# Which of the free PSUM banks a product takes

## The chip, the cores and the metric

The kernel runs on one core of one Trainium2 chip. The metric is the device time of one execution in microseconds (us); the median of three runs is what a change is judged by. PE is TensorE's matmul stream, PEld its weight loads, DVE is VectorE, ACT is ScalarE, POOL is GpSimd, SP is SyncE, which issues nearly all DMAs. "L749" is line 749 of the kernel.

## The reference

A depthwise convolution over time with 7 taps, the tap weights a softmax shared by the 24 channels of each of 8 heads, is followed by RMS norm and a gated feed-forward layer. All is float32.

```python
x: (8, 4096, 192), weight: (8, 7), w_gate, w_val: (192, 1536), w_out: (1536, 192)
w = softmax(weight)                                  # over the 7 taps, per head
out[b, s, h, g] = sum_k w[h, k] * x_pad[b, s + k, h, g]    # 6 zero rows ahead of each batch row
x = out.reshape(32768, 192)
xn = x / sqrt(mean(x * x, -1) + 1e-6) * rms_g
g = xn @ w_gate
y = ((g * sigmoid(g)) * (xn @ w_val)) @ w_out         # (32768, 192)
```

## The kernel before

**Tiling.** The 32768 tokens are cut into 32 pairs of 2 x 512 tokens, each a stretch of 1024 tokens of one batch row. The hidden width of 1536 is cut into 4 units of 3 x 128 columns. The input products save multiplications by a Winograd-like scheme: sums of blocks of the input (XSUM, into the tile `xc`) and sums of blocks of the weights (WSUM, into `wf`) are multiplied, and the results are put together afterwards. The gate and the value matrices are worked on at once, on partitions 0 to 63 (half 0) and 64 to 127 (half 1) of the contraction; each product is one matmul on either half. The output products use a second scheme of this kind (OUTS) with three accumulators, X, Y and Z.

**Pair 0 and the others.** Pair 0 is computed plainly (`plain` and `outer`), while the weights are made ready. Pairs 1 to 31 are computed by the class `Pair`, and each of them goes through the same list of words, ORDER, written out by hand. The words set the order of the instructions on every engine: "p2" issues two more steps of PE's list of products, and a word such as "VR1.0.0" one operation: V, A, G and D stand for DVE, ACT, POOL and a DMA, R1 is the action, then half and unit. A "-" at the end means that the operation belongs to the pair before. So each engine's queue is fixed; the engines wait for each other by semaphores alone.

**The products of a unit.** PE's list for a pair is CHAINS, 240 matmul instructions of L749 (a float32 product takes two on each half), and then OUTS, 672 matmul instructions of L878. A unit has a number of running values v; each is accumulated in one PSUM bank per half. Three of them (4, 1, 5) are begun by a product[...]. The others (0, 2, 3) are begun by a fork ("F"): ACT or DVE copies value 1, 4 or 5 into another bank, and later products add to the copy. In unit 0 of a pair the first six products go to values 4, 1, 5, 4, 0, 4, in this order, on half 0 and half 1 in turn. The first reads block 5 of `xc`, the second block 9, the third a block of `xb` (the fetched input), the fourth `xc` block 4, the fifth block 7, the sixth block 8.

**Banks.** There are 8 PSUM banks of 512 columns, 4 for each half. For each half `free` lists the banks that are free, the one freed longest ago first. The set `whole` holds the banks that a matmul has written in all 512 columns since they were last begun. [...] The output accumulators X (half 0) and Z (half 1) are begun by matmuls that write 384 columns, so `open` strikes their banks off `whole`. `pick(h, full)` goes through the list for the first bank that is whole (or is not), and takes the first of the list if there is none:

```python
i = next((i for i in free[h] if ((h, i) in whole) == full), free[h][0])
```

A bank is given back when the last operation on it is issued: `leave` after a result (R, L773), a Silu (G) or a product with the gate (M); `part_tap` (L444) after the last tap of one of the three pieces of the convolution of a later pair, which run in PSUM too; `close` after Z is added to its tile (C21, L924), or after X or Y was transposed into the output tile (T12 and T11, two transposes each of L893). The instruction that next writes the bank waits for that operation.

**Where one pair meets the next.** The last DVE words of a pair are: C22 (L924, reads X at an earlier stage of its sum), the last tap of conv piece 1 (L444), T22, the block sum X2 (L667), C21 (the last reader of Z), a reduction of the norm (L470 to L472), the block sums X5, X8 and X10 (L667, into `xc` blocks 4, 7 and 9), T12. POOL's are the block sums X7, X3, X1, X6 (L667) and the norm's power (L476 to L482). Then come the next pair's first two product steps, and after them T11 (DVE, out of Y), and on POOL the block sums X9 and X4 of that pair (into `xc` blocks 8 and 3) and the norm's scaling (L497).

Of the kernel before, what the change touches and what calls it, by code (L numbers as in the profile page):

```python
# [19 lines left out]
def kernel(  # L20
# [650 lines left out]
    free = [[0, 1, 2, 3], [0, 1, 2, 3]]  # L671

    def bank(half, i):
        return ps[half * 4 + i]
# [4 lines left out]
    whole = {(h, i) for h in range(2) for i in range(4)}  # L679

    def pick(h, full):

        i = next((i for i in free[h] if ((h, i) in whole) == full), free[h][0])
        free[h].remove(i)
        return i
# [8 lines left out]
    def emit(until):  # L694
        while line and line[0][0] < until:
            heapq.heappop(line)[2]()
# [26 lines left out]
    class Unit:  # L723
# [3 lines left out]
            self.bk, self.tl = {}, {}  # L727

        def new(self, v, h, product=False):
            i = self.bk[v, h] = pick(h, not product)  # L730
            if product:
                whole.add((h, i))
            assert (h, i) in whole
            return bank(h, i)[:]
# [228 lines left out]
    def plain(hts):  # L963


        groups = [(u, g, f) for u in range(NU) for g in (1, 0) for f in range(NF)]
        groups[0 : 2 * NF] = [(0, g, f) for f in range(NF) for g in (1, 0)]
        held = {}

        def products():  # L970
            for u, g, f in groups:
                if len(hts) <= u:
                    hts.append(big.tile([P, 2, NF, T], F32, name="ht"))
                bks = held[u, g, f] = [free[h].pop(0) for h in range(2)]
                for k in range(KP):
                    for h in range(2):
                        nc.tensor.matmul(  # L977
                            out=bank(h, bks[h])[:], lhsT=wf[u][HALF[h], k * NF + f, :],
                            rhs=xb[HALF[h], g, k, :], start=(k == 0), stop=(k == KP - 1),
                            skip_group_check=True,  # L980
                        )
                yield

        def silus():
            for i in groups:
                sg = tiles.pop(0)
                nc.scalar.activation(out=sg[:], in_=bank(0, held[i][0])[:], func=AF.Silu)
                held[i].append(sg)
                yield

        def values():
            for u, g, f in groups:
                *bks, sg = held.pop((u, g, f))
                nc.vector.tensor_tensor(
                    out=hts[u][:, g, f, :], in0=bank(1, bks[1])[:], in1=sg[:], op=ALU.mult
                )
                tiles.append(sg)
                for h in range(2):
                    free[h].append(bks[h])
                yield  # L1000

        return products(), silus(), values()
# [118 lines left out]
    p, sl, v = plain(hts)  # L1121
# [44 lines left out]
    later(out_sums(), *[base + 2600 + 60 * i for i in range(4 * NM)])  # L1166
    emit(float("inf"))

    order = [w for row in ORDER for w in row.split()]
    past = None  # L1170
    for p in range(1, PAIRS + 1):
# [42 lines left out]
```

## Time and profile before

| | |
|---|---|
| median of 3 runs | 2642.21 us (2641.62 to 2646.78) |
| the profiled execution | 2638.08 us |
| its span, first to last instruction | 2636.2 us |
| granted TensorE clock | 0.997 of full |
| busy: PE, PEld | 2581.8 us, 1878.4 us |
| busy: DVE, POOL, ACT | 2271.7, 2091.1, 1614.4 us |
| L749 (input products) | 7440 matmul instructions, about 0.59 us each, overlapping |
| L878 (output products) | 17360 matmul instructions, 0.27 us (128 columns) or 0.38 us (256 columns) each, overlapping |

The page gives, for one execution, the busy time of each engine, the span in 40 slices, the chain of work that ended last, and the costliest groups of instructions. Matmuls are pipelined, so the durations of single ones overlap and their sum is more than the time; what matters is where PE stood idle and who ended the idle time. In the timeline a line gives the start, the busy time, the engine, the line, the operation, what it writes and reads, the shape, how many were merged ("x8"), and in square brackets the idle time ahead and the instruction that ended it. In the list of waits a line gives who waited for whom, the total in us, how many times, and the longest.

### The profile page before, as it was taken

Reading aid. Unit: us, or ns where it says so; the run is one execution under the profiler, and the core shown is the slowest. Engines: PE = TensorE matmul, PEld = TensorE weight load, DVE = VectorE, ACT = ScalarE, POOL = GpSimd, SP = SyncE. Lnnn points to the kernel's source line nnn. Section 1 sums busy time; section 2 is a strip of 40 time slices with the busy share of each in tenths; the row PEclk is TensorE's granted clock in tenths of the full one; section 3 lists DMA queues with packets and bytes.
Section 4 is the critical chain, followed back from the end, with each engine's and each line's share of the span. In section 5 each row is a group of like instructions: output and inputs, shape, how many; then the busy total and the mean of one; then the engine's idle time right before and its main releaser. Section 6 shows DMA issues by size and latency. Waiting matters only on the chain.

```text
span 2636.2 us, 71036 instructions
## 1 busy us (share of the span) xinstructions
PE 2581.8 (98%) x29002; PEld 1878.4 (71%) x29002; DVE 2271.7 (86%) x3606; ACT 1614.4 (61%) x2964; POOL 2091.1 (79%) x1693
## 2 busy tenths in 40 slices
PE   6999999999999999999999999999999999999998
PEld 3677777776777776777776777767777777777676
DVE  8988889888888888889888888888898888988875
ACT  5375556765556765557755567655577555676554
POOL 3987788877888777888787887777887778887776
PEclk9999999999999999999999999999999999999999
DMA  6312321323312223213233222233132232132210
GB/s 142 60 35 56 63 50 39 62 38 63 63 39 49 50 51 63 55 34 62 39 63 63 42 46 54 47 63 60 33 57 47 55 63 45 44 62 38 50 38 14
DMA packets 510660, 138.01 MB, mean 52 GB/s; under 512 B 482301, under 2 KB 484861, under 8 KB 510206
## 3 DMA queue, kind: packets, MB, share of 16 engines
q1 hardware_dynamic: 509772, 133.44, 26.7%
q8 instruction: 227, 3.72, 0.6%
q14 instruction: 101, 0.82, 0.1%
q10 hardware_dynamic: 560, 0.03, 0.0%
HBM read 83.87 MB, written 49.55 MB: 51 GB/s over the span
## 4 chain that ended last, share of the span: by engine, by line
PE 89%; DVE 6%; issue 2%; POOL 1%; SPq 1%; DMA 1%; ACT 0%; DVEq 0%; POOLq 0%
PE ps L749 61%; PE ps L878 27%; DVE xc L667 1%; DVE s L470 1%; DVE o_sb L893 1%; PE ps L977 1%; POOL wf L349 1%; DVE tls L924 1%; DVE y L444 0%; SPq L1115 0%; DMA x<-in_x_dram 0%; DVE y L405 0%; POOL wo_sb L311 0%; SPq L217 0%; DMA ht<-in_moe_w_val_dram 0%
## 5 line engine op out<-in xcount | busy, mean ns | idle before, releaser
L749 PE MATMUL ps<-xc,wf 64*128 64x512 f32 x4960 | 1249.7, 592 | 17.3 <-DVE o_sb L893 16.3
L749 PEld LDWEIGHTS ps<-xc,wf 64*128 64x128 f32 x4960 | 764.2, 186 | 319.5 <-issue 117.3
L749 PE MATMUL ps<-xb,wf 64*128 64x512 f32 x2480 | 707.7, 589 | 0.0
L705 ACT ACTIVATE tls<-ps 128x512 f32<-128x512 f32 (+1 forms) x636 | 365.6, 589 | 384.7 <-PE ps L878 204.0
L793 POOL TENSOR_TENSOR ht<-ht,tile 128x512 f32<-128x512 f32 x295 | 374.8, 1277 | 277.5 <-ACT tile L786 276.1
L705 ACT ACTIVATE tile<-ps 128x512 f32<-128x512 f32 x697 | 400.0, 594 | 277.2 <-PE ps L749 166.9
L749 PEld LDWEIGHTS ps<-xb,wf 64*128 64x128 f32 x2480 | 394.7, 187 | 138.4 <-issue 38.1
L705 ACT ACTIVATE ps<-ps 128x512 f32<-128x512 f32 (+1 forms) x651 | 366.9, 578 | 53.1 <-PE ps L878 38.8
L906 POOL TENSOR_TENSOR early<-ht 128x512 f32<-128x512 f32 x279 | 378.2, 1360 | 4.9
L793 POOL TENSOR_TENSOR ht<-ht,tls 128x512 f32<-128x512 f32 x201 | 254.9, 1275 | 72.4 <-ACT tls L786 70.5
L878 PE MATMUL ps<-ht,wo_sb 128*32 128x256 f32 (+1 forms) x6944 | 308.7, 326 | 0.0
L773 DVE TENSOR_TENSOR tile<-ps,tile 128x512 f32<-128x512 f32 x373 | 255.0, 687 | 56.1 <-PE ps L749 53.5
L444 DVE SCALAR_TENSOR_TENSOR ps<-xh,tp,ps 128x512 f32<-128x512 f32 x435 | 301.7, 746 | 1.0
L878 PEld LDWEIGHTS ps<-ht,wo_sb 128*32 128x32 f32 x6944 | 215.0, 110 | 93.0 <-POOL ht L793 23.5
L878 PE MATMUL ps<-ht,x 128*32 128x256 f32 (+1 forms) x5952 | 249.2, 326 | 0.2 <-issue 0.2
L906 POOL TENSOR_TENSOR ht<-ht 128x512 f32<-128x512 f32 x186 | 247.5, 1345 | 0.0
L786 ACT ACTIVATE tile<-tile 128x512 f32<-128x512 f32 x373 | 232.9, 629 | 12.5 <-DVE tile L773 12.5
L878 PEld LDWEIGHTS ps<-ht,x 128*32 128x32 f32 x5952 | 191.7, 110 | 52.1 <-issue 0.7
L773 DVE TENSOR_TENSOR ht<-ps,tls 128x512 f32<-128x512 f32 x311 | 212.0, 682 | 0.0
L773 DVE TENSOR_TENSOR ht<-ps,tile 128x512 f32<-128x512 f32 x309 | 210.5, 681 | 0.0
L773 DVE TENSOR_TENSOR tls<-ps,tls 128x512 f32<-128x512 f32 x247 | 169.5, 686 | 28.2 <-PE ps L749 26.1
L878 PE MATMUL ps<-early,x 128*32 128x256 f32 (+1 forms) x4464 | 192.8, 326 | 0.0
(129 smaller groups left out, 3167.2 us busy)
## 6 DMA issues: line engine op xcount, KB each, us to landing
xb<-xd SPq DMA_DIRECT2D x124, 384.0 KB
xd<-yn SPq DMA_DIRECT2D x248, 96.0 KB
out_dram<-o_sb SPq DMA_DIRECT2D x186, 128.0 KB
xh<-in_x_dram SPq DMA_DIRECT2D x192, 105.0 KB
xh<-in_x_dram SPq DMA_DIRECT2D x56, 98.4 KB
ht<-in_moe_w_gate_dram SPq DMA_DIRECT2D x12, 192.0 KB
ht<-in_moe_w_val_dram SPq DMA_DIRECT2D x12, 192.0 KB
tls<-in_moe_w_out_dram SPq DMA_DIRECT2D x8, 192.0 KB
```

Of the source, the lines that this page charges most:

```text
L349: nc.gpsimd.tensor_tensor(out=t[:, d, :], in0=t[:, a, :], in1=t[:, b, :], op=ALU.add if op == "add" else ALU.subtract,)
L444: nc.vector.scalar_tensor_tensor(out=dst, in0=xk, scalar=w, in1=at, op0=ALU.mult, op1=ALU.add)
L470: nc.vector.tensor_reduce(out=ss[:], in_=sq, axis=AX.X, op=ALU.add)
L667: e.tensor_tensor(out=xc[:, d, :], in0=x_op(a), in1=x_op(b), op=ALU.add)
L705: nc.scalar.activation(out=dst, in_=src, func=AF.Copy, scale=float(s))
L749: nc.tensor.matmul(out=self.new(v, h, True) if first else self.old(v, h), lhsT=wf[self.u][HALF[h], WAT[i], :], rhs=x_op(XOP[i])[HALF[h]], ...
L773: nc.vector.tensor_tensor(out=self.hv(v) if h else t[:], in0=self.old(v, h), in1=t[:], op=plus(s))
L786: nc.scalar.activation(out=t[:], in_=src[:], func=AF.Silu)
L793: engine[eng].tensor_tensor(out=self.hv(v), in0=src, in1=t[:], op=ALU.mult)
L878: nc.tensor.matmul(out=self.bank(b)[i * Q : (i + 1) * Q, at : at + n], lhsT=left, rhs=cols, start=fresh, stop=True, skip_group_check=True, ...
L893: nc.vector.transpose(out=to[:, n, lo:hi], in_=src[:, lo * Q : hi * Q].rearrange("p (b e) -> p b e", e=Q),)
L906: engine[eng].tensor_tensor(out=dst, in0=a, in1=b, op=op)
```

## The change

A product that begins value 4 or 1 takes the head of the free list, whatever is marked. A product that begins value 5 goes on looking for a bank that isn't whole; so do the output accumulators X and Z and the pieces of the convolution, which call `pick` themselves. Forks go on asking for a whole bank. Once, after pair 0 and ahead of pair 1, the free lists are sorted so that the banks that are not whole stand first; the order within the two groups stays.

```diff
@@ class Unit
         def new(self, v, h, product=False):
-            i = self.bk[v, h] = pick(h, not product)
+            if product and v != 5:
+                i = free[h].pop(0)
+            else:
+                i = pick(h, not product)
+            self.bk[v, h] = i
             if product:
                 whole.add((h, i))
             assert (h, i) in whole
@@ ahead of the loop over the pairs
     later(out_sums(), *[base + 2600 + 60 * i for i in range(4 * NM)])
     emit(float("inf"))
 
+    for h in range(2):
+        free[h].sort(key=lambda i: (h, i) in whole)
     order = [w for row in ORDER for w in row.split()]
     past = None
     for p in range(1, PAIRS + 1):
```

## The prediction

> **What bounds the kernel now.** I read the page first, then TensorE's list of waits, then the timelines of TensorE (PE), its weight loads (PEld), VectorE (DVE) and GpSimd (POOL) around two borders between pairs: one near 303 us, one near 382 us.
>
> ```profile
> span 2636.2 us, 71036 instructions
> ...
> PE 2581.8 (98%) x29002; PEld 1878.4 (71%) x29002; DVE 2271.7 (86%) x3606; ACT 1614.4 (61%) x2964; POOL 2091.1 (79%) x1693
> ```
>
> PE is busy for all but 54 us. A gain must come out of those 54 us, or from shorter matmuls, which the change does not touch. The list of what PE waited for (total, times, longest):
>
> ```profile
> PE ps L749 <- DVE o_sb L893: 16.3, 19, 0.9
> ...
> PE ps L878 <- issue: 1.7, 4, 1.0
> ```
>
> The first line is the only wait that recurs in the steady loop: a matmul of line 749 waits for a transpose of line 893. The large remaining waits (15.7, 5.5 and 3.0 us, each once) are in the start. PE's timeline at a border that waits and at one that doesn't:
>
> ```profile
> 300.12 2.13 PE L878 MATMUL ps<-ht,wo_sb 128*32 128x256 f32 x48
> 303.16 1.99 PE L749 MATMUL ps<-xc,wf 64*128 64x512 f32 x8 [0.90 <-DVE o_sb L893]
> ...
> 382.63 1.99 PE L749 MATMUL ps<-xc,wf 64*128 64x512 f32 x8
> ```
>
> Reading the idle time ahead of the first L749 matmul at all 30 borders from the same view: 18 have 0.81 to 0.94 us (16.1 us in all), one 0.20, three 0.04 to 0.06, eight nothing; sum 16.4 us. A border without a wait comes mostly 79.47 us after the one ahead, a border with one about 80.45 us. DVE just ahead of both borders:
>
> ```profile
> 294.59 0.56 DVE L924 TENSOR_TENSOR tile<-ps,tile 128x384 f32<-128x384 f32 x1 [2.31 <-PE ps L878]
> ...
> 296.27 1.72 DVE L667 TENSOR_TENSOR xc<-xb,xc 128x512 f32<-128x512 f32 x1
> ...
> 301.77 0.69 DVE L667 TENSOR_TENSOR xc<-xc 128x512 f32<-128x512 f32 x1
> 302.38 1.16 DVE L893 STREAM_TRANSPOSE o_sb<-ps 128x256 f32<-128x256 f32 x4
> 306.12 0.69 DVE L769 TENSOR_TENSOR tls<-ps,tls 128x512 f32<-128x512 f32 x1 [2.58 <-PE ps L749]
> ...
> 375.04 0.56 DVE L924 TENSOR_TENSOR tile<-ps,tile 128x384 f32<-128x384 f32 x1 [1.06 <-PE ps L878]
> ...
> 376.72 0.71 DVE L667 TENSOR_TENSOR xc<-xb,xc 128x512 f32<-128x512 f32 x1
> ...
> 381.82 0.63 DVE L893 STREAM_TRANSPOSE o_sb<-ps 128x256 f32<-128x256 f32 x2
> ```
>
> At 294.59 DVE has waited for PE's bank X; then it has a fixed row of work that ends with T12, the transpose out of X. Of the four transposes at 302.38 two are T12; at 381.82 they stand alone and take 0.63, so T12 ends at 303.01. PE was ready at 303.16 - 0.90 = 302.26. The waiting border is 1.0 us later because one sum (X2) takes 1.72 instead of 0.71 us. POOL shows why:
>
> ```profile
> 296.15 1.29 POOL L667 TENSOR_TENSOR xc<-xb,xc 128x512 f32<-128x512 f32 x1
> ...
> 376.82 1.76 POOL L667 TENSOR_TENSOR xc<-xb,xc 128x512 f32<-128x512 f32 x1
> ```
>
> Whichever of the two sums starts first runs at its own pace, the other is held.
>
> [...] the third product's load (304.52) is 0.43 us ahead of its matmul (304.95).
>
> **The change, part by part.** I followed both free lists through a pair. On half 0 a pair starts with banks last freed by unit 3's R2, by conv piece 0, by conv piece 2 and by T12 (bank X, the only one not whole); on half 1 with those freed by R2, by conv piece 1 and by C21 (bank Z, not whole), and T11's a little later.
>
> 1. *Before*, every product prefers the bank that isn't whole: product 4, the first matmul of the pair, takes X on half 0 and so waits for T12, the latest event of all. *After*, product 4 takes R2's bank, product 1 the conv piece's, product 5 takes X and Z. Fork 0 takes what it took. From there on all banks are whole, both rules take the head of the list, and each later bank has the same releaser as before: only bank numbers differ. So six bank choices per border move, 30 times; no matmul, copy, transpose or DMA is added, removed or moved in any queue.
>
> 2. *The wait removed.* R2's bank was freed tens of us earlier. Removed: all 16.4 us.
>
> 3. *Where the stall goes: product 5.* Its first matmul is third product, 1.79 us after the first (304.95 - 303.16), and its weight load, where a wait can hold it, 1.39 us after:
>
> ```profile
> 303.13 0.33 PEld L749 LDWEIGHTS ps<-xc,wf 64*128 64x128 f32 x4 [1.14 <-issue]
> 303.67 0.22 PEld L749 LDWEIGHTS ps<-xc,wf 64*128 64x128 f32 x2 [0.21 <-issue]
> 304.10 0.22 PEld L749 LDWEIGHTS ps<-xc,wf 64*128 64x128 f32 x2 [0.21 <-issue]
> 304.52 0.22 PEld L749 LDWEIGHTS ps<-xb,wf 64*128 64x128 f32 x2 [0.21 <-issue]
> ```
>
> With the first product at 302.26 the load comes at 303.65. T12 ends at 303.01 and was seen by the load at 303.13, so 0.52 us are left: cost 0. If T12 were later than that, every product queued behind on PE, and through them ACT's copies, would slip by the difference.
>
> 4. *What is late next: X10.* Product 1 reads xc's slot 9, which X10 (301.77, just ahead of T12) writes. Until now the wait for T12 covered it. It ends at 302.46 and is visible at 302.58; product 1's load comes at 302.26 + (303.67 - 303.13) = 302.80. 0.22 us left: cost 0, and the thinnest cover.
>
> 5. *Further on.* The sixth product reads what POOL's next sum writes (303.73 + 1.26 = 304.99); it starts at 302.26 + 5 x 0.86 = 306.56, its load 0.43 earlier: 1.1 us left. T11's bank is free at 303.54, ahead of the end of product 1 on which fork 0 waits. DVE waits 2.58 us for PE at 306.12, so it still falls in step with PE, 0.9 us earlier. POOL's chain shrinks from a 0.88 us wait to none, and its next wait is 5.0 us. All three follow PE, so the gain stays.
>
> 6. *Waits to be added.* One wait at product 4 becomes up to three (products 4, 1, 5). A separate semaphore instruction on PE takes 51 ns in this trace: from 0 to 30 x 3 x 0.05 = 4.6 us. The loads sit idle 0.21 us between one another: I take 0.
>
> 7. *The sort.* At pair 1 the lists are 3, 1, 2, 0 with only 3 whole; sorted they are 1, 2, 0, 3, which gives pair 1 the banks it had. Host work: 0.
>
> Sum: -16.4 us against the profiled execution's 2638.08 us (span 2636.2), so about 2621.7 there. That execution is 4.1 us below the median shown, so against the median: 2642.2 - 16.4 = 2625.8, said as 2626. Differences under 0.2% (5.3 us) can hardly be told from no change.
>
> **Unknown at both ends.** Four pairs lose about 1 us to "issue" in the output products (the second wait line; those pairs take 80.45 to 80.8 us with no or almost no wait at the border). Two of them follow the 8 borders without a wait, two the 18 with one. If the rate without waits (1 in 4) holds for all, it is 7.5 instead of 4: +3.5 us; if they vanish, -4 us.
>
> **Rivals.**
> - *The wait comes back in part* at product 1 or 5, because DVE has drifted by more than 0.22 or 0.52 us. [...] At 0.2 to 0.5 us in 20 pairs it gives back 4 to 10 us: 2630 to 2636.
> - *The wait moves elsewhere in the pair*, DVE or POOL setting the pace: 2640 to 2643. For it: DVE 86%, POOL 79% busy. Against: both wait for PE in every pair, and seven borders already come 79.5 us after the one ahead with no wait at either place.
> - *Slower:* PE, never pausing at the border, outruns its instruction supply in the output products. Place: line 878; price about 1.0 us a time, 4 times in 30 now. It cancels the gain at 16 more pairs and is slower by 0.2% from 22 more: all 26 remaining ones would give about 2652. For it: the small excess noted above; against: 18 pauses of 0.9 us didn't prevent it either.
> - That the change doesn't do what it says would need X to be whole when product 4 picks; opening X always strikes it off, so I give this nothing apart.
>
> **How the numbers follow.** Full gain 0.80 (own range 2622 to 2630), partial 0.08, moved 0.06, slower 0.06. Faster by over 0.2%: 0.88, within: 0.06, slower: 0.06. The range 2622 to 2636 takes in the full gain with both ends of the unknowns and most of the partial case.
>
> **What would show it.** Right: no L749 wait on L893 left; every border 79.5 us apart save a few with "issue"; X2 still 1.72 us in many pairs without effect; PE busy as before, span about 2620. Wrong at step 3: L749 waits on L893 at the third product. Wrong at step 4: L749 waits on L667. Wrong at step 5: new PE waits inside the pair. The prediction fails if DVE at the border comes over 0.5 us later relative to PE than in this trace.

## The result and the profile after

Median 2624.88 us (2624.07 to 2626.45, four runs) against 2641.91 us of the kernel before on the same chip: ratio 0.9932, 95% interval 0.992 to 0.9943, 17.0 us less. Run again beside later experiments: 2624.53 against 2643.72 us, ratio 0.9925 (0.9909 to 0.9942). The profiled execution took 2624.07 us, 14.0 us less than that of before.

In the changed kernel the lines behind the edit stand four further down: L749 is L753, L878 is L882, L893 is L897, L924 is L928. L882, as L878 before, is 20832 matmul instructions (672 in each of 31 pairs); the 17360 of the table above leaves out its smaller groups. First the head of the page after:

```profile
span 2622.2 us, 71005 instructions
...
PE 2579.8 (98%) x29002; PEld 1858.8 (71%) x29002; DVE 2268.0 (86%) x3606; ACT 1614.9 (62%) x2964; POOL 2091.7 (80%) x1693
```

PE's busy time is within 2 us of what it was (2581.8); the span is 14.0 us shorter. In the list of PE's waits (total, times, longest) these are all that is left of L753 and L882:

```profile
PE ps L882 <- issue: 1.9, 5, 0.8
...
PE ps L753 <- DVE xc L667: 0.9, 1, 0.9
```

The wait for the transposes, 16.3 us in 19 places, is gone altogether, and no other that recurs has come in (the one wait for L667 stood in the list before too, with 0.8 us). The chain that ended last says the same. By engine, before:

```profile
PE 89%; DVE 6%; issue 2%; POOL 1%; SPq 1%; DMA 1%; ACT 0%; DVEq 0%; POOLq 0%
```

and after:

```profile
PE 95%; POOL 1%; DMA 1%; DVE 1%; SPq 1%; issue 0%; ACT 0%; DVEq 0%; POOLq 0%
```

At the borders DVE has left the chain: its 6% was the way from C22's wait through T12 to product 4, and nearly all that is left of it lies in the start. Now a border at which the sum X2 takes 1.73 us, one of POOL's sums having begun 0.11 us ahead of it (a held border, from here on; at the six borders where X2 starts 0.08 to 0.13 us ahead of that sum it takes 0.67 to 0.73 us), in PE's timeline, then in that of the weight loads:

```profile
301.80 1.70 PE L882 MATMUL ps<-ht,wo_sb 128*32 128x128 f32 x40
303.43 1.99 PE L753 MATMUL ps<-xc,wf 64*128 64x512 f32 x8
305.25 1.02 PE L753 MATMUL ps<-xb,wf 64*128 64x512 f32 x4
306.11 1.45 PE L753 MATMUL ps<-xc,wf 64*128 64x512 f32 x6
```

```profile
303.43 0.30 PEld L753 LDWEIGHTS ps<-xc,wf 64*128 64x128 f32 x4 [0.20 <-issue]
303.97 0.19 PEld L753 LDWEIGHTS ps<-xc,wf 64*128 64x128 f32 x2 [0.23 <-DVE xc L667]
...
304.83 0.19 PEld L753 LDWEIGHTS ps<-xb,wf 64*128 64x128 f32 x2 [0.24 <-DVE o_sb L897]
```

Product 1's load (303.97) now names X10, and product 5's (304.83) names T12, as the prediction worked out. Both come at their due times, by which I mean the times at which they come when nothing holds them: 0.54 and 1.40 us after the first product. So neither waits; idle times of 0.23 and 0.24 us are the stream's usual ones. At all 30 borders these loads come within 0.01 us of these times. DVE and POOL there:

```profile
295.84 0.56 DVE L928 TENSOR_TENSOR tile<-ps,tile 128x384 f32<-128x384 f32 x1 [2.30 <-PE ps L882]
...
297.53 1.73 DVE L667 TENSOR_TENSOR xc<-xb,xc 128x512 f32<-128x512 f32 x1
...
303.04 0.69 DVE L667 TENSOR_TENSOR xc<-xc 128x512 f32<-128x512 f32 x1
303.65 1.16 DVE L897 STREAM_TRANSPOSE o_sb<-ps 128x256 f32<-128x256 f32 x4
306.42 0.69 DVE L773 TENSOR_TENSOR tls<-ps,tls 128x512 f32<-128x512 f32 x1 [1.61 <-PE ps L753]
```

```profile
297.42 1.29 POOL L667 TENSOR_TENSOR xc<-xb,xc 128x512 f32<-128x512 f32 x1
...
307.46 2.92 POOL L497 TENSOR_TENSOR yn<-y,s 128x1536 f32<-128x1536 f32 x1
```

X2 still takes 1.73 us and T12 is as late as ever: it ends at 303.65 + 0.63 = 304.28, now 0.85 us *after* the first product. DVE's next wait for PE is 1.61 us (2.58 before), POOL's wait of 0.88 us ahead of L497 is used up, and its next one is 4.93 us (5.01 before).

Where the 14.0 us of the profile come from: the waits at the borders are worth 16.4 us; 2.1 us are lost again in the start, and 0.3 us, on balance, elsewhere. The start, up to the first L753 matmul at 142.9 us (140.8 before), lies ahead of all the bank choices that changed. In the ten profiles of the experiments it takes 141.9 to 143.4 us under either rule, so the early start belongs to that one execution of the kernel before and not to the rule. The medians differ by 17.0.

### The profile page after: what moved, and what is told of

It is laid out like the page before. It is cut to its first block, busy times and chain, and to the rows that moved or that the text cites. A ratio compares the mean times of both kernels' runs of the same rounds, so it can differ in the third digit from the quotient of the medians.

```text
span 2622.2 us, 71005 instructions
## 1 busy us (share of the span) xinstructions
PE 2579.8 (98%) x29002; PEld 1858.8 (71%) x29002; DVE 2268.0 (86%) x3606; ACT 1614.9 (62%) x2964; POOL 2091.7 (80%) x1693
## 4 chain that ended last, share of the span: by engine, by line
PE 95%; POOL 1%; DMA 1%; DVE 1%; SPq 1%; issue 0%; ACT 0%; DVEq 0%; POOLq 0%
PE ps L753 62%; PE ps L882 33%; POOL wf L349 1%; PE ps L981 1%; DMA xh<-in_x_dram 0%; SPq L1119 0%; SPq L217 0%; DMA x<-in_x_dram 0%; POOL wo_sb L311 0%; DVE y L420 0%; DMA ht<-in_moe_w_val_dram 0%; DVE xc L667 0%; DVE ht L998 0%; DMA ht<-in_moe_w_gate_dram 0%; POOL xc L310 0%
## 5 line engine op out<-in xcount | busy, mean ns | idle before, releaser
L753 PE MATMUL ps<-xc,wf 64*128 64x512 f32 x4960 | 1253.8, 592 | 0.9 <-DVE xc L667 0.9
L753 PEld LDWEIGHTS ps<-xc,wf 64*128 64x128 f32 x4960 | 753.5, 186 | 315.5 <-issue 92.9
L753 PE MATMUL ps<-xb,wf 64*128 64x512 f32 x2480 | 711.2, 589 | 0.0
L753 PEld LDWEIGHTS ps<-xb,wf 64*128 64x128 f32 x2480 | 389.7, 187 | 146.5 <-issue 41.1
L882 PE MATMUL ps<-ht,wo_sb 128*32 128x256 f32 (+1 forms) x6944 | 309.5, 326 | 0.0
L882 PEld LDWEIGHTS ps<-ht,wo_sb 128*32 128x32 f32 x6944 | 215.2, 110 | 93.2 <-POOL ht L797 22.7
L882 PE MATMUL ps<-ht,x 128*32 128x256 f32 (+1 forms) x5952 | 249.9, 326 | 0.6 <-issue 0.6
L882 PEld LDWEIGHTS ps<-ht,x 128*32 128x32 f32 x5952 | 190.1, 110 | 54.7 <-issue 2.3
L882 PE MATMUL ps<-early,x 128*32 128x256 f32 (+1 forms) x4464 | 193.1, 326 | 0.1
```

Source lines behind the costliest of these rows:

```text
L753: nc.tensor.matmul(out=self.new(v, h, True) if first else self.old(v, h), lhsT=wf[self.u][HALF[h], WAT[i], :], rhs=x_op(XOP[i])[HALF[h]], ...
L882: nc.tensor.matmul(out=self.bank(b)[i * Q : (i + 1) * Q, at : at + n], lhsT=left, rhs=cols, start=fresh, stop=True, skip_group_check=True, ...
```

## The experiments

Each time is set against the kernel before on the same chip. Where the changed kernel did not run beside it, "over the changed kernel" sets the distances of the two from the kernel before side by side.

**One half at a time: h0_only and h1_only.** The new rule on one half of the banks, the old one on the other.

```diff
-            if product and v != 5:
+            if product and v != 5 and h == 0:     # h0_only; h == 1 in h1_only
```

> The new rule on half 0 only; on half 1 every product prefers the bank that is not whole, as before, so its product 4 takes Z. My theory (the wait is for T12, on X's bank, half 0): the whole gain, 16 to 17 us below the kernel before, no L749 wait on L893 (here a shifted line). Rival A (the gain comes from Z and half 1): no change. Rival B (the gain comes from spreading the products over banks in general): about half, 8 us.

> The new rule on half 1 only; on half 0 product 4 still takes X. My theory: no change against the kernel before (within 1 us), 18 or 19 waits for T12's transposes, some 16 us. Rival A: the whole gain, 17 us. Rival B: about 8 us.

Measured: half 0 alone 2625.75 against 2644.89 us, ratio 0.9927 (0.9911 to 0.9944), 19.1 us less, and no wait of L753 for L897. Half 1 alone 2643.98 us, ratio 1.0 (0.9992 to 1.0009), with this line in PE's list of waits (23 where my theory had 18 or 19; five of them are under 0.75 us):

```profile
PE ps L753 <- DVE o_sb L897: 18.9, 23, 0.9
```

The whole gain lies on half 0, in X's bank and T12. Z's bank and C21, which half 1 concerns, are worth nothing that can be measured, and so is spreading the products over the banks on that half; early_before, below, has the gain with no spreading at all. Both kernels keep the sort of the free lists, so h1_only shows that the sort alone is worth nothing either.

**How late T12 may be: x_to_1.** Product 1 takes X's bank, 0.86 us earlier than product 5.

```diff
-            if product and v != 5:
+            if product and v != 1:
```

> Product 1 instead of product 5 takes the bank that is not whole; 4 and 5 take the head of the list. Product 1's weight load comes 0.54 us after the first product, T12 is visible 0.87 to 0.97 us after it in the 14 to 18 borders with the held sum. My theory: 0.33 to 0.43 us of wait there, 5 to 8 us of the gain lost: 9 to 12 us below the kernel before. Rival C (it is enough that the first product doesn't take X): the whole gain, 17 us. Rival D (T12 is late by far more than 0.5 us once PE no longer waits for it): more than 10 us lost.

Measured 2628.19 us (2624.72 to 2631.08), ratio 0.9935 (0.992 to 0.9949): 16.7 us below the kernel before. My theory's loss of 5 to 8 us did not come; by the ratio nearly the whole gain is there, as rival C had it. The median is still 2.4 us above that of h0_only on this chip; the trace has 0.7 us of loss at the borders and 7.0 us of "issue" waits, against 4.8. The wait that my theory spoke of is in the trace. Weight loads, then matmuls, at a held border:

```profile
782.68 0.30 PEld L753 LDWEIGHTS ps<-xc,wf 64*128 64x128 f32 x4 [0.20 <-issue]
783.58 0.30 PEld L753 LDWEIGHTS ps<-xc,wf 64*128 64x128 f32 x4 [0.60 <-DVE o_sb L897]
```

```profile
782.68 2.03 PE L753 MATMUL ps<-xc,wf 64*128 64x512 f32 x8
784.54 1.02 PE L753 MATMUL ps<-xb,wf 64*128 64x512 f32 x4
```

Product 1's load comes 0.90 us after the first product instead of 0.54, and is held by T12. Yet the third product starts 1.86 us after the first, where the changed kernel has 1.82: of 0.36 us, 0.04 remain. When nothing holds them the loads run 0.43 us ahead of their matmuls (product 5's in the changed kernel 1.39 and 1.82 us after the first product), and the two passes of a product (its first and its second matmul on each half) have a load each (x2), 0.43 us apart. When the first load is held, the loads of both passes go out together (x4 in 0.30 us), and the matmul doesn't need the old lead: it starts 0.07 us into a load of 0.18 us. In the traces of four_after and x1_twice, below, load and matmul of the held product start together (787.60 and 787.60, 784.40 and 784.40).

**T12 twice: twice_after and twice_before.** T12's transposes are issued twice, so X's bank is free one repeat later.

```diff
-                self.turn(self.bank(b), 0, int(act[2]) - 1)
+                for _ in range(2 if b == "X" else 1):
+                    self.turn(self.bank(b), 0, int(act[2]) - 1)
                 self.close(b)
```

> The changed kernel with T12's two transposes issued twice (the same values written again), so X's bank is free about 0.58 us later. My theory: in the borders with the held sum T12 is visible 1.45 to 1.55 us after the first product, product 5's load comes at 1.39: 0.06 to 0.16 us in 14 to 18 borders, 1 to 3 us over the changed kernel, 14 to 16 us below the kernel before. Rival D (there is no spare time at product 5): 0.58 us in 14 to 30 borders, 8 to 17 us over the changed kernel.

> The kernel before with T12's two transposes issued twice. My theory (product 4 waits for T12 with no spare time): 0.53 to 0.58 us at all 30 borders, 16 to 17 us slower than the kernel before. Rival E (DVE catches the lost time up elsewhere in the pair, or the wait seen at the border is only partly T12's): under 8 us.

The changed kernel with it: 2624.28 us, ratio 0.992 (0.9905 to 0.9935), no loss: product 5's load is held past its due time at 14 borders, by 0.07 us at most, and no product is late for it. My theory's 1 to 3 us did not come, nor rival D's 8 to 17. The kernel before with it: 2659.18 against 2642.35 us, ratio 1.0064 (1.0049 to 1.0079), 16.8 us slower, and all 30 borders wait:

```profile
PE ps L749 <- DVE o_sb L893: 33.5, 30, 1.5
```

The same 0.53 us of DVE work at the same place costs 0.56 us a border under the old rule (16.8 / 30; 0.43 to 0.70 by the interval) and nothing that can be measured under the new one. That is the change in one comparison, and rival E is out.

**T12 earlier: early_before and early_after.** T12 moves up in DVE's order, ahead of X8 and X10, under either rule.

```diff
-        ... VX5 p2 VX8 p2 VX10 p1 Gpow VT12 p2
+        ... VX5 p2 VT12 VX8 p2 VX10 p1 Gpow p2
```

> The kernel before with T12 moved up in DVE's order, from behind X10 to behind X5; the old bank rule. T12 then ends near 301.75 on the scale of the border at 303 us, ahead of PE's 302.26: product 4 waits no more. X8 and X10 end 0.58 us later, X10 visible at about 303.1, product 1's load at 302.80. My theory: 0.3 to 0.4 us of wait for L667 at 18 borders, 5 to 7 us of the gain missing: 10 to 12 us below the kernel before. Rival F (the wait at product 4 is for something else that ends together with T12): no change. Rival G (X10 has ample time): the whole gain, 17 us.

> The changed kernel with T12 moved up in the same way. My theory: product 5 has no need of it, and X10, now later, holds product 1: the same time as the kernel before with T12 moved up (within 1 us), so 5 to 7 us over the changed kernel, 10 to 12 us below the kernel before. Rival G: the time of the changed kernel.

Measured 2626.68 against 2642.35 us, ratio 0.9938 (0.9922 to 0.9955), with the old rule; 2624.90 us, ratio 0.9936 (0.9921 to 0.9951), with the new one. The two are the same within 2 us, as my theory had it, but at the level of the changed kernel, not 5 to 7 us above. No wait for L893 is left with the old rule, so it was T12 and nothing else that product 4 waited for: rival F is out. Weight loads, then matmuls, of early_before at a held border:

```profile
303.03 0.30 PEld L749 LDWEIGHTS ps<-xc,wf 64*128 64x128 f32 x4 [0.20 <-issue]
303.88 0.31 PEld L749 LDWEIGHTS ps<-xc,wf 64*128 64x128 f32 x4 [0.55 <-DVE xc L667]
```

```profile
303.03 1.99 PE L749 MATMUL ps<-xc,wf 64*128 64x512 f32 x8
304.86 1.02 PE L749 MATMUL ps<-xb,wf 64*128 64x512 f32 x4
```

X10 does hold product 1's load, for 0.31 us over its due time (0.85 instead of 0.54), and again the products after it are not late: the third starts 1.83 us after the first, where the changed kernel has 1.82, and no border of either kernel loses more than 0.03 us. So moving one operation in DVE's order does what the change does: what matters is that the *first* product needn't wait. It has no load running ahead that could absorb a wait (its load and its matmul start together, 303.43 and 303.43 in the changed kernel).

**The size of what is absorbed: after_again, four_after, x1_twice.** Two kernels in which the hold is long enough to cost, with the changed kernel beside them. four_after is twice_after with `range(4 ...`; x1_twice is twice_after with `v != 1`.

> The changed kernel itself once more, as the base for the two beside it: 16 to 18 us below the kernel before.

> The changed kernel with T12's two transposes issued four times (the same values written again): each repeat adds 0.53 us, so T12 is visible 2.56 us after the first product in the held borders, 1.54 in the others; product 5's weight load is due at 1.39, its matmul at 1.82. Theory H (a late weight load is absorbed for about 0.40 us, since the load is issued ahead of its matmul): 0.77 us of wait at some 18 borders, none at the others: 12 to 15 us over the changed kernel. Theory I (the wait costs from the load's due time on, as worked out in the prediction): 1.17 us at 18 borders and 0.15 at the others: 21 to 24 us over the changed kernel.

> Product 1 takes X's bank (product 5 the head of the list), and T12's transposes are issued twice: visible 1.51 us after the first product in the held borders, 0.48 in the others; product 1's weight load is due at 0.54, its matmul at 0.96. Theory H: 0.57 us at some 18 borders, 9 to 11 us over the changed kernel. Theory I: 0.97 us at some 18 borders, 16 to 18 us over the changed kernel, no better than the kernel before.

Against 2643.72 us before: the changed kernel 2624.53, four_after 2639.61 (ratio 0.9983, 0.9977 to 0.999), x1_twice 2637.70 (0.9977, 0.9968 to 0.9986); 15.1 and 13.2 us over the changed kernel. For four_after that is at the edge of theory H and far below theory I; for x1_twice it lies between the two, 2 us above H and 3 below I. The traces decide. PE at a held border of four_after, with the load that it waits for:

```profile
785.13 1.99 PE L753 MATMUL ps<-xc,wf 64*128 64x512 f32 x8
787.60 1.13 PE L753 MATMUL ps<-xb,wf 64*128 64x512 f32 x4 [0.48 <-DVE o_sb L897]
788.56 1.88 PE L753 MATMUL ps<-xc,wf 64*128 64x512 f32 x8
```

```profile
787.60 0.30 PEld L753 LDWEIGHTS ps<-xb,wf 64*128 64x128 f32 x4 [1.31 <-DVE o_sb L897]
```

Product 5's load goes out 2.47 us after the first product instead of 1.39, 1.08 late; the fourth product (788.56) comes at 3.43 instead of 2.68 (306.11 - 303.43), 0.75 late. The sixth is 0.75 late too. So 0.33 us are absorbed. In x1_twice:

```profile
783.00 1.13 PE L753 MATMUL ps<-xc,wf 64*128 64x512 f32 x4
784.40 1.13 PE L753 MATMUL ps<-xc,wf 64*128 64x512 f32 x4 [0.27 <-DVE o_sb L897]
785.37 1.02 PE L753 MATMUL ps<-xb,wf 64*128 64x512 f32 x4
```

```profile
784.40 0.30 PEld L753 LDWEIGHTS ps<-xc,wf 64*128 64x128 f32 x4 [1.10 <-DVE o_sb L897]
```

the load comes 1.40 us after the first product instead of 0.54, 0.86 late, and the products from the third on 0.54: 0.32 absorbed. With x_to_1 (0.36 late, 0.04 left) that is the same figure three times, and all the traces agree: of the 119 loads of products 1 and 5 that X10 or T12 held by over 0.02 us in these kernels, the 43 held by up to 0.32 us delay the products from the fourth on by nothing, and each of the others by its own lateness less 0.32 us. The lines show where the 0.32 comes from. The load's lead is 0.43 us; but a product whose load has no lead takes 1.13 us (787.60, 784.40, as the first of the border does at 783.00), where one with a lead takes 1.02 (305.25), since its second pass follows after 0.53 us and not 0.43. The lead less these 0.11 us is 0.32. Why the passes then stand further apart isn't shown.

Summed over the 30 borders of the traces the delay is 14.1 us for four_after and 9.9 for x1_twice. "Issue" waits are 1.7 us (five) and 5.8 us (seven), against 4.4 us (six) in the changed kernel beside them. Together that makes 11.4 and 11.3 us over the changed kernel; the profiled executions are 11.8 and 12.0 us apart. The medians are 1 to 3 us further apart: the profiled execution of the changed kernel is the slowest of its four, that of four_after among its fastest.

## Why the prediction was right

*Steps 1 and 2* (which products take which banks; 16.4 us removed) hold: product 5's load names T12, no L753 wait on the transposes is left, 19 of 30 borders come 79.50 us after the one ahead, and the medians differ by 17.0. h0_only and h1_only show that the gain lies on X's half alone, and twice_before and early_before that T12 is what product 4 waited for. The predicted 2625.8 lies 0.9 us from the measured median. So close a hit is luck in part: the runs of the changed kernel alone are 2.4 us apart, those of the kernel before 5.3 us, and the repetition beside later kernels gave 19.2 us of gain.

*Step 3* (the stall goes to product 5, with 0.52 us to spare) has the right sign and place and the wrong size, twice over. T12 is visible to a load (0.12 us after its end) 0.97 us after the first product, not 0.87, so 0.43 us remain to the load's due time. Most of this comes from reading PE's readiness off the end of the last output matmul: the first product starts 0.07 us ahead of that end (303.43 against 301.80 + 1.70 = 303.50). And the due time is not where it begins to cost: another 0.32 us are absorbed, so that the true cover is about 0.75 us. The two errors had opposite signs, and the change itself put neither to the test. Beyond it the price is as worked out: each further tenth of a microsecond costs a tenth at every held border (four_after: 1.08 us late, 0.75 = 1.08 - 0.33 lost).

*Step 4* (X10 is the thinnest cover, 0.22 us): X10 ends 0.30 us after the first product; with the 0.12 us to be seen that leaves 0.12 us to the load and some 0.44 us to a cost. early_before and early_after used it up without loss. So the step put the distance to the due time too high (0.22 instead of 0.12) and the distance to a cost too low (0.22 instead of 0.44), and my expectations for x_to_1 and both early kernels, which count the cost from the due time in the same way, were wrong by it.

*Step 5* (all other engines fall in step with PE again): shown by DVE's wait shrinking from 2.58 to 1.61 us and POOL's from 0.88 to nothing, with no new wait of PE. Its due time for the sixth product is misread: that product starts 4.51 us after the first in the kernel before and its load 4.48, not 0.43 earlier than it. That leaves some 0.5 us more than the 1.1 us of the step, so nothing hangs on it.

*Step 6* (added waits at 0): no trace of a cost. Separate semaphore instructions of the input products are 97 in the profile before and 97 after, of 51 ns each, and the changed loads sit idle as long as their neighbours (0.23 and 0.24 us). *Step 7* (the sort at 0): h1_only has it and gains nothing.

*The rivals.* Part of the wait coming back and the wait moving elsewhere: neither is in the trace, though X2 takes over 1.4 us at 19 of the 30 borders (18 before). The slower one, PE outrunning its instructions: "issue" waits on the output products are 5 in the profile after (1.9 us) and 4 before (1.7 us). The three kernels that still pause at the border (the kernel before, h1_only, twice_before) have 1.7 to 2.7 us of them, the nine others 1.7 to 7.0 us, 4.2 in the mean. So this rival may be right by some 2 us; with so few profiles that is not shown. Of the nine, leaving out the two whose holds cost something at the borders (four_after, x1_twice), the shortest and the longest span, 2622.2 and 2629.2 us, have 1.9 and 7.0 us of these waits. What causes them was not tried and stays open.

## What to carry to other kernels

When a buffer goes free late, give it to the consumer that comes some steps later rather than to the first one: nothing has to be made faster, and a wait on the critical path becomes slack, as far as that consumer's cover reaches (here about 0.75 us). The list of waits tells who is last; the worth is the sum of that wait, provided that the other engines still wait for this one further on. And after the move, look at the next thing that the old wait covered.

## What the runs showed that was not expected

In this stream a weight load held past its due time costs nothing for the first 0.32 us (measured as 0.36 - 0.04, 1.08 - 0.75 and 0.86 - 0.54), and from there on as much as it is late: it runs 0.43 us ahead of its matmul, and a product that loses this lead takes 0.11 us longer. The first product after the output products has no such cover: there the kernel before paid its wait in full, and 0.53 us more of DVE work cost 0.56 us a border.
